# Fifth batch's x from two heads by 576 columns, weights of two steps converted in halves, new order

## Chip, cores and metric

One Trainium2 chip (trn2), one core. The metric is the device time of one execution in microseconds, median of three runs.

## What is computed

Attention for 8 batches of 8 heads (sequence 576, head size 64), with a softmax over the head size for q and over the sequence for k, then one MLP over all 4608 tokens:

```python
q_s = softmax(q, axis=-1); k_s = softmax(k, axis=2)     # max, exp, sum, division
kv = einsum('bhsd,bhse->bhde', k_s, v)
attn_out = einsum('bhsd,bhde->bhse', q_s, kv)
x = attn_out.transpose(0, 2, 1, 3).reshape(4608, 512)
h = x @ w_in                                            # 512 -> 2048
g = s * relu(h) ** 2 + b
out = g @ w_out                                         # 2048 -> 512
```

## The kernel before

All loops are unrolled. Each piece of work is a Python generator (a "stream") that yields an Op before each instruction group, with the engine, a modelled cost and what it needs, takes, frees and gives. A table, FIRST, is the order of the whole program: each number is the index of the stream whose next operation is issued. So FIRST sets the order on TensorE (PE), VectorE (DVE), ScalarE (ACT), GpSimd (POOL) and in SyncE's (SP) DMA queue, and every engine executes its own list in order.

The MLP runs in steps t = 16 * batch pair + f, over 16 slices f of the 2048. A step makes h (PE, L1868), relu (ACT, L1895), gh and gl (the high and the low part of g in fp32r; gl on DVE, L1905, L1914, L1921) and adds the products acc into the output (PE, L1942). Products are made with a high and a low part of each operand. From step 48 on, some products are combined Strassen-like: `early_sums` adds quarters of w_in (sum on DVE, stored as s_kept), and `differences_0` makes t1 to t4 (zone and t, DVE L1099 to L1110) from x of batches 4 and 6.

The attention runs in between. A pair pr is two units u = 2 pr + i of two heads each; four units are one batch, so batch 4 has u = 16 to 19, pairs 8 and 9. For batches 2 and above, `q_late` makes q's softmax and its transposed form qT, `kv_late` makes kv, `x_late` makes x. A pair is direct if its batch is below DIRECT: its q is cast to high and low parts (qhl or spare, all 128 partitions, one unit for both heads at once), kv becomes a block matrix of both heads, and x takes six matmuls (high by high, high by low, low by high; 320 and 256 columns, L934). For a pair that isn't direct, each head's high and low parts are packed into 128 partitions, with two DMAs qhl/spare<-qT (L840); x then takes one matmul per head and column part, and the two halves of partitions are added: a copy on ACT (L919), a sum on DVE (L923). `kv_late` normalises with two products (L884) for a direct pair and with four (L890) for another.

Batches 4 and 6 (PARK) are written to DRAM once x is known (xpark<-y) and come back as w<-xpark. `conv_w(f)` converts the weights of slice f to high and low parts by three operations of ACT and three of DVE, interleaved (low, clamp of st, prelu of st, low, cast w, difference w; L368 to L385), for w_in and w_out together (128x1024) or, for slice 0, apart (128x512). `fill` and `unused` (L2080) are matmuls of the identity with no use for the result, that the order table puts between products early on. mb is a per-column maximum, which goes through DRAM: sb (DVE) is stored as maxima and loaded as mb<-maxima for the k part of a batch.

For a pair that isn't direct, the branch of `x_late` that batch 4 now takes is:

```python
yield Op("PE", 0.57, begin(pr) + OFF_PE, needs=needs + free_x, take=["big", "sm"], gives=[f"xp{u}"], late=WAIT)
parts = [(xp[:, h, 0:L], xq[:, h * M:(h + 1) * M]) for h in range(2)]
for h in range(2):
    for a, n in enumerate((NT, NQ)):
        nc.tensor.matmul(parts[h][a], kvhl[:, h], qs[:, h, a, 0:n], start=True, stop=True)
for a in range(2):
    yield Op("ACT", (0.68, 0.67)[a], due, take=() if a else ["tmp"])
    for h in range(2):
        halves([(a, parts[h][a])], h)
for a in range(2):
    yield Op("DVE", (0.84, 0.7)[a], due, free=["big", "sm"] if a else (), gives=[f"y{u}"] if a else ())
    for h in range(2):
        sums_([(a, parts[h][a])], h)
```

Of the kernel before, what the change touches and what calls it, by code (L numbers as in the profile page):

```python
# [26 lines left out]
def attention_moe(ctx: ExitStack, tc: tile.TileContext, q, k, v, w_in, w_out, s, b, out):  # L27
# [6 lines left out]
    NFC = FF // P  # L34
# [7 lines left out]
    DUE_C0 = -60.0  # L42
# [101 lines left out]
    ON_ACT = (-1.0, -1.0, -1.0, -1.0, -1.0, 1.0, -1.0, -1.0, -1.0, 1.0, -1.0, 1.0, -1.0, 1.0, -1.0, 1.0)  # L144
    KN_ON = ('ACT', 'ACT', 'ACT', 'DVE')
    QF_ON = ('ACT', 'DVE', 'ACT', 'DVE', 'DVE', 'ACT', 'DVE', 'DVE')
    LESS_ON, OVER_ON = (1, 1, 1, 1, 1, 1, 1, 1), (1, 1, 1, 1, 0, 0, 0, 0)
    KT_IN = ("big", "acc") * 2
    BLOCKS_ON = [(("ACT", 1.03), ("DVE", 0.56))[i] for i in (1, 1, 0, 0)]
    WARM = 40  # L150
    IN_BIG = (1,)

    DUE_K = (-104.0, -52.5, -76.0, -79.5, 6.5, 28.5, 13.0, 38.5)
    DUE_Q = (-81.5, 70.0, -73.5, -18.0, 13.5, 2.0, -131.0, -33.5)
    DUE_V = (-26.0, -150.5, -207.0, -210.5)
    LATE_PR = (4, 5, 6, 7, 8, 9, 10, 11, 12, 13, 14, 15)
# [6 lines left out]
    PAIRS, ALONE, DIRECT = 3, 5, 5  # L163
# [19 lines left out]
    _, acc_low = banks("ps_acc0", "left")  # L183
    accs_open, acc_top = banks("ps_acc1", "left")
    two_banks, bigs = banks("ps_big", "right")
    free_accs = [acc_low, acc_top]
# [1957 lines left out]
```

## Time and profile before

| | |
|---|---|
| runs | 831.95, 830.03, 830.07 us |
| median | 830.07 us |
| profiled execution | 828.33 us, with a span of 826.5 us |
| PE busy | 818.7 us (99%) |
| DVE busy | 679.8 us (82%) |
| ACT busy | 531.0 us (64%) |
| granted TensorE clock | 1.00 (mean) |

The span goes from the first instruction to the last; the profiled execution has 1.8 us around it. Matmuls are pipelined, so a busy PE needn't be at its peak.

### The profile page before, as it was taken

To read this page: it belongs to the slowest core of one execution; us is meant where nothing else is said; L and a number is where in the kernel's file an instruction comes from. 1 tells how busy PE (TensorE), PEld (TensorE's weight loads), DVE (VectorE), ACT (ScalarE), POOL (GpSimd) and SP (SyncE) were. 2 spreads that over 40 slices of the span, in tenths; PEclk is the share of its full clock that TensorE was granted. 3 is DMA by queue.
4 is the path that set the end of the run, shared out by engine and by line. 5 is a ranking of instruction groups with operands and counts; after the bars stand their busy time and mean duration, and the time that the engine had idled before them with its cause. 6 is when DMAs were issued, how large, how long until landed. Compare 5 with 4: busy or idle time off the path is not lost.

```text
span 826.5 us, 12989 instructions
## 1 busy us (share of the span) xinstructions
PE 818.7 (99%) x4590; PEld 688.2 (83%) x4590; DVE 679.8 (82%) x1157; ACT 531.0 (64%) x931; POOL 25.3 (3%) x67
## 2 busy tenths in 40 slices
PE   8999999999999999999999999999999999999997
PEld 7787888888888888888888888888888888888997
DVE  6999997898888999989886898875555968789991
ACT  6899955455365456868886455765653457778950
POOL 5201000000000000000000000000000000000000
PEclk9999999999999999999999999999999999999999
DMA  9859235655896897888989987755469644453303
GB/s 313 314 174 364 60 90 146 197 136 192 257 322 185 261 211 227 230 263 233 252 260 313 327 281 222 226 182 175 147 244 345 228 161 149 176 178 115 110 20 102
DMA packets 152485, 173.41 MB, mean 210 GB/s; under 512 B 68836, under 2 KB 117476, under 8 KB 152292
## 3 DMA queue, kind: packets, MB, share of 16 engines
q1 hardware_dynamic: 151796, 171.99, 66.6%
q8 instruction: 36, 0.59, 0.3%
q10 hardware_dynamic: 624, 0.59, 0.2%
q14 instruction: 29, 0.24, 0.1%
HBM read 115.34 MB, written 43.04 MB: 192 GB/s over the span
## 4 chain that ended last, share of the span: by engine, by line
PE 93%; DVE 3%; DMA 2%; issue 1%; ACT 1%; SPq 0%; POOL 0%; ACTq 0%; DVEq 0%; POOLq 0%
PE acc L1942 35%; PE q L1323 24%; PE h L1868 13%; PE half_U L1764 6%; PE qa L1323 4%; PE half_A L1764 2%; DMA st<-in_moe_w_out_dram 2%; PE kv L474 1%; PE qa L1764 1%; PE xp L934 1%; PE b L1764 1%; PE b L474 1%; PE b L946 1%; PE kT L522 1%; PE xp L644 0%
## 5 line engine op out<-in xcount | busy, mean ns | idle before, releaser
L1942 PE MATMUL acc<-w,gh 128*128 128x512 f32 x880 | 273.5, 392 | 0.0
L1942 PEld LDWEIGHTS acc<-w,gh 128*128 128x128 f32 x880 | 162.6, 188 | 33.0 <-DVE o L1955 0.2
L1942 PE MATMUL acc<-w,gl 128*128 128x512 f32 x440 | 172.0, 391 | 0.1
L1868 PE MATMUL h<-x,w 128*128 128x512 f32 x576 | 143.8, 392 | 0.0
L1868 PEld LDWEIGHTS h<-x,w 128*128 128x128 f32 x576 | 106.8, 188 | 23.0 <-ACT r L1895 0.9
L1942 PEld LDWEIGHTS acc<-w,gl 128*128 128x128 f32 x440 | 82.6, 188 | 19.1 <-DVE gl L1921 1.1
L1323 PE MATMUL q<-w,w 128*128 128x512 f32 x376 | 95.6, 391 | 0.0
L1323 PEld LDWEIGHTS q<-w,w 128*128 128x128 f32 x376 | 70.0, 188 | 15.1 <-ACT r L1430 0.4
L1895 ACT ACTIVATE r<-h 128x512 f32<-128x512 f32 x48 | 28.6, 596 | 52.0 <-PE h L1868 49.7
L1430 ACT COPY zone<-q 128x512 f32<-128x512 f32 x32 | 18.7, 585 | 30.8 <-PE q L1323 29.8
L1432 DVE TENSOR_TENSOR zone<-q,zone 128x512 f32<-128x512 f32 x32 | 22.1, 690 | 19.0 <-ACT zone L1430 14.2
L1323 PE MATMUL q<-x,w 128*128 128x512 f32 x144 | 36.8, 391 | 0.0
L1323 PE MATMUL qa<-x,w 128*128 128x512 f32 x144 | 36.6, 389 | 0.0
L1323 PEld LDWEIGHTS qa<-x,w 128*128 128x128 f32 x144 | 27.0, 188 | 5.6
L1323 PEld LDWEIGHTS q<-x,w 128*128 128x128 f32 x144 | 26.8, 188 | 5.7
L1764 PE MATMUL half_U<-w 128*128 128x256 f32 x168 | 28.1, 283 | 0.0
L919 ACT COPY y<-b 64x320 f32<-64x320 f32 (+1 forms) x48 | 18.9, 394 | 11.4 <-PE b L946 10.6
L923 DVE TENSOR_TENSOR y<-b,y 64x320 f32<-64x320 f32 (+1 forms) x48 | 21.7, 453 | 5.4 <-ACT y L919 4.5
L1764 PEld LDWEIGHTS half_U<-w 128*128 128x128 f32 x168 | 24.1, 191 | 0.6
L1323 PE MATMUL q<-w,s 128*128 128x512 f32 x96 | 24.5, 391 | 0.0
L799 ACT ACTIVATE qe<-area 128x640 f32<-128x640 f32 x22 | 17.2, 787 | 10.3 <-DVE area L795 9.4
L1544 ACT CAST gh<-t 128x512 fp32r<-128x512 f32 x14 | 8.7, 624 | 23.1 <-PE acc L1942 23.1
(341 smaller groups left out, 1656.4 us busy)
## 6 DMA issues: line engine op xcount, KB each, us to landing
w<-w_kept SPq DMA_DIRECT2D x56, 512.0 KB, 5.5
st<-in_moe_w_in_dram SPq DMA_DIRECT2D x16, 512.0 KB, 8.0
st<-in_moe_w_out_dram SPq DMA_DIRECT2D x16, 512.0 KB, 8.4
w_kept<-w SPq DMA_DIRECT2D x16, 512.0 KB, 5.9
zone<-s_kept SPq DMA_DIRECT2D x16, 512.0 KB, 4.3
turned<-area SPq DMA_DIRECT2D x24, 320.0 KB, 3.5
qT<-turned SPq DMA_DIRECT2D x48, 160.0 KB, 3.5
area<-in_q_dram SPq DMA_DIRECT2D x14, 512.0 KB, 4.8
```

Source lines behind the costliest of these rows:

```text
L474: nc.tensor.matmul(kv[h * D:(h + 1) * D, i], kt[:, i, h, n], vt(2 * i + h, n), start=(n == 0), stop=(n == NT - 1))
L799: nc.scalar.activation(qe, qt_, AF.Exp)
L919: nc.scalar.copy(y[half[h], at[a]], x[half[1 - h]])
L923: nc.vector.tensor_tensor(out=y[half[h], at[a]], in0=x[half[h]], in1=y[half[h], at[a]], op=ALU.add)
L1323: nc.tensor.matmul(BANK[where], w(l)[:, c * P:(c + 1) * P], xs[m][:, c], start=k in (0, 1, 3) and n == 0, stop=n == 5, skip_group_check=True)
L1430: nc.scalar.copy(row(), BANK["U"])
L1432: nc.vector.tensor_tensor(out=row(), in0=BANK[("A", "B", "B")[n]], in1=row(), op=ALU.add)
L1544: nc.scalar.copy(gh, r)
L1764: nc.tensor.matmul(bank(where, j), g[:, js], w_, start=first and (j % 2 == 0 or k == 3) and n == 0, stop=bool(low), skip_group_check=True)
L1868: nc.tensor.matmul(hp_, w[:, j, c, :], x[:, c, :], start=(c == 0 and i == 0), stop=(c == NP - 1 and i == 2))
L1895: nc.scalar.activation(r, hp_, AF.Relu)
L1942: nc.tensor.matmul(acc[blk, j // 2][:, j % 2], g[:, js], w_, start=(f == 0 and i == 0), stop=(f == NFC - 1 and i == 2))
```

## The change

DIRECT goes from 5 to 4, so that batch 4's four units take the branch quoted above, with the two DMAs per unit and the four normalisation products per pair. HALVED lists the slices 1 and 2, whose weights are now converted in two halves: w_in first, w_out in a stream of its own at the end of the list (indices 669 and 670 in FIRST); its end waits until the first half has been read. The two banks for the products acc are taken in the other order. FIRST is rewritten to match: the order early on and in the stretch of batch 4; the rest has the same sequence. Of the table only its first lines are shown.

```diff
     FIRST = (
-        0, 18, 18, 0, 0, 18, 18, 20, 21, 46, 52, 19, 46, 46, 47, 2, 52, 46, 52, 3, 53, 46, 22, 47, 53, 52, 47, 52, 48, 46, 3, 68, 52, 53, 47, 52, 48, 4, 49, 47,
-        54, 4, 48, 55, 52, 54, 49, 68, 52, 55, 53, 49, 48, 29, 68, 49, 48, 29, 53, 49, 54, 53, 52, 29, 54, 52, 53, 69, 1, 29, 69, 55, 54, 53, 54, 29, 24, 52, 31, 53,
...
+        0, 18, 18, 0, 18, 0, 18, 20, 21, 46, 52, 19, 46, 46, 47, 2, 52, 46, 52, 22, 53, 46, 47, 53, 52, 47, 52, 3, 48, 46, 3, 68, 52, 53, 47, 52, 48, 49, 47, 24,
+        55, 48, 54, 52, 55, 49, 68, 52, 54, 53, 49, 48, 29, 68, 49, 48, 69, 29, 54, 53, 52, 49, 1, 53, 29, 54, 52, 4, 29, 53, 52, 4, 69, 55, 54, 23, 53, 54, 29, 55,
+        31, 53, 2, 29, 5, 31, 54, 53, 55, 69, 6, 72, 55, 54, 56, 5, 1, 31, 54, 53, 56, 1, 669, 57, 55, 54, 31, 25, 72, 32, 57, 55, 31, 54, 55, 56, 32, 669, 32, 72,
...
@@ -148,6 +149,7 @@
+    HALVED = (1, 2,)
@@ -160,7 +162,7 @@
-    PAIRS, ALONE, DIRECT = 3, 5, 5
+    PAIRS, ALONE, DIRECT = 3, 5, 4
@@ -183,7 +185,7 @@
-    free_accs = [acc_low, acc_top]
+    free_accs = [acc_top, acc_low]
@@ -373,7 +375,7 @@
-        yield Op("DVE", 1.13 * two + 0.03 * (n == 1), due, free=["w"] if last else (), gives=[f"w{f} {some.stop} read"], two=True)
+        yield Op("DVE", 1.13 * two + 0.03 * (n == 1), due, needs=[f"w{f} 1 read"] if last and n == 1 else (), free=["w"] if last else (), gives=[f"w{f} {some.stop} read"], two=True)
@@ -2092,7 +2094,7 @@
-            + [conv_w(0, slice(0, 1), DUE_C0), conv_w(0, slice(1, 2))] + [conv_w(f, slice(0, 2)) for f in range(1, NFC)]
+            + [conv_w(0, slice(0, 1), DUE_C0), conv_w(0, slice(1, 2))] + [conv_w(f, slice(0, 2 - (f in HALVED))) for f in range(1, NFC)]
@@ -2108,7 +2110,7 @@
-            + [exit_(n) for n in range(3)] + [exit_21()] + [exit_last(j) for j in (0, 2, 3)],
+            + [exit_(n) for n in range(3)] + [exit_21()] + [exit_last(j) for j in (0, 2, 3)] + [conv_w(f, slice(1, 2)) for f in HALVED],
```

On PE, in the early part of the program (h are products of a step, acc its output products, fill the matmuls without use, xp x of the first batch, qT and kT transposes), before:

```order
L1868 MATMUL h_406<-x_330,w_379 128x512 x3
L2080 MATMUL fill_444<-ident 128x128 x5
L644 MATMUL xp_450<-early,kvf 128x256
L644 MATMUL xp_450<-early,kvf 128x320
L2080 MATMUL fill_471<-ident 128x128 x9
L1868 MATMUL h_406<-x_330,w_379 128x512 x6
L2080 MATMUL fill_495<-ident 128x128 x4
L1868 MATMUL h_500<-x_330,w_468 128x512 x12
L2080 MATMUL fill_530<-ident 128x128 x6
L1942 MATMUL acc_0_537<-w_379,gh_491 128x512 x2
L1942 MATMUL acc_0_537<-w_379,gl_492 128x512
```

and after:

```order
L1870 MATMUL h_413<-x_329,w_386 128x512 x3
L2082 MATMUL fill_458<-ident 128x128 x3
L646 MATMUL xp_462<-early,kvf 128x256
L646 MATMUL xp_462<-early,kvf 128x320
L1870 MATMUL h_413<-x_329,w_386 128x512 x3
L2082 MATMUL fill_488<-ident 128x128 x9
L1870 MATMUL h_413<-x_329,w_386 128x512 x3
L1870 MATMUL h_505<-x_329,w_455 128x512 x6
L673 MATMUL kT_520<-ident,misc 128x128 x2
L1870 MATMUL h_505<-x_329,w_455 128x512 x6
L1870 MATMUL h_537<-x_329,w_503 128x512 x12
L1944 MATMUL acc_0_566<-w_386,gh_510 128x512 x2
```

Fill goes from four groups of 5, 9, 4 and 6 to two groups of 3 and 9; h of the second and third step come ahead of the first acc products.

On DVE, where the last parked unit of batch 4 is made (y its halves' sum, xp and xq the products in two buffers, sb the maxima that SP stores; gl_2935 belongs to step 41), before:

```order
L704 STREAM_TRANSPOSE misc<-misc 128x256
L709 TENSOR_REDUCE sb<-misc 128x8
L778 TENSOR_REDUCE qm_2950<-area 128x10
L795 TENSOR_TENSOR area<-area,qm_2950 128x640
L1910 TENSOR_SCALAR r_2933<-r_2933,sb 128x512
L1187 TENSOR_TENSOR sum_2937<-w_988 128x512
L802 TENSOR_REDUCE qs_2983<-qe_2975 128x20
L1914 TENSOR_TENSOR gl_2935<-r_2933,gh_2934 128x512
```

and after (gl_3044 belongs to step 42; lines are two higher than before):

```order
L706 STREAM_TRANSPOSE misc<-misc 128x256
L1919 SCALAR_TENSOR_TENSOR r_3042<-h_3002,sb,r_3042 128x512
L806 SCALAR_TENSOR_TENSOR qs_3037<-qs_3037 128x2x5
L811 RECIPROCAL qr_3060<-qs_3037 128x20
L804 TENSOR_REDUCE qs_3065<-qe_3030 128x20
L711 TENSOR_REDUCE sb<-misc 128x8
L925 TENSOR_TENSOR y_3050<-xp_3024,y_3050 64x320 x2
L1923 SCALAR_TENSOR_TENSOR gl_3044<-r_3042,sb,gh_3043 128x512
L925 TENSOR_TENSOR y_3050<-xq_3025,y_3050 64x256 x2
L806 SCALAR_TENSOR_TENSOR qs_3065<-qs_3065 128x2x5
```

sb has moved from ahead of gl of step 41 to between the gl of steps 41 and 42, right ahead of the four sums of the last y, with the gl of step 42 among these; before, y needed no operation of DVE.

In SP's queue, from the stores of batch 4 to the load w<-xpark for the second half of it, before:

```order
L430 DMA xleft<-misc 128x2x64
L714 DMA maxima_2973<-sb 128x4x2
L992 DMA xpark<-y_3009 128x4x64 x2
L1222 DMA zone<-s_kept 128x1024
L992 DMA xpark<-y_2964 128x4x64 x2
L719 DMA mb_3054<-maxima_2973 128x1024
L1074 DMA w_576<-xpark 128x1024
```

and after:

```order
L994 DMA xpark<-y_2969 128x4x64 x2
L716 DMA maxima_3075<-sb 128x4x2
L1032 DMA w_kept<-w_1042 128x1024
L994 DMA xpark<-y_3050 128x4x64 x2
L721 DMA mb_3113<-maxima_3075 128x1024
L432 DMA xleft<-misc 128x2x64
L1076 DMA w_588<-xpark 128x1024
```

mb<-maxima stands ahead of the load w<-xpark as before, but xleft<-misc moved behind it, to just ahead of w<-xpark, and the store of maxima stands behind the stores of one parked unit and ahead of those of the other, where it was ahead of both.

## Rows read from the trace of the kernel before

**Rows 1.** The page: busy time, share of the span, instructions of the engines.

```profile
PE 818.7 (99%) x4590; PEld 688.2 (83%) x4590; DVE 679.8 (82%) x1157; ACT 531.0 (64%) x931; POOL 25.3 (3%) x67
```

**Rows 2.** The chain of waits: share of the span by engine.

```profile
PE 93%; DVE 3%; DMA 2%; issue 1%; ACT 1%; SPq 0%; POOL 0%; ACTq 0%; DVEq 0%; POOLq 0%
```

**Rows 3.** Stretches: us, busy time of each engine, granted clock, DMA share, GB/s.

```profile
20.00:30.00 10.00, 9.72 (x65) 7.42 (x60) 9.96 (x18) 9.04 (x16) 5.74 (x9) 1.00 0.72 235
80.00:90.00 10.00, 9.95 (x45) 7.90 (x44) 10.00 (x14) 9.53 (x13) 0.40 (x2) 1.00 0.25 49
290.00:300.00 10.00, 10.00 (x46) 8.29 (x45) 9.75 (x16) 4.23 (x7) 0.00 (x0) 1.00 1.06 194
300.00:310.00 10.00, 10.00 (x46) 8.29 (x45) 8.73 (x14) 7.15 (x11) 0.21 (x2) 1.00 0.80 235
```

**Rows 4.** Timeline of PE, an x group: start, length, instructions.

```profile
255.26 0.96 PE L934 MATMUL xp<-qhl,spare 128*128 128x320 f32 x6
256.06 0.85 PE L1868 MATMUL h<-x,w 128*128 128x512 f32 x3
```

**Rows 5.** Groups by line: minimum, median, maximum ns, first and last start.

```profile
L923 DVE TENSOR_TENSOR y<-b,y x48: 406/437/496, 336.3 to 617.7; 64x320 f32<-64x320 f32 x24, 64x256 f32<-64x256 f32 x24
L919 ACT COPY y<-b x48: 363/396/425, 334.8 to 616.8; 64x320 f32<-64x320 f32 x24, 64x256 f32<-64x256 f32 x24
L982 ACT COPY y<-xp x4: 583/587/587, 259.3 to 288.1; 128x512 f32<-128x512 f32 x4
L837 ACT CAST qhl<-qhl x6: 723/726/727, 318.5 to 558.8; 64x640 fp32r<-64x640 f32 x6
```

**Rows 6.** Timeline of DVE around 281 to 319 us, idle time in brackets.

```profile
281.81 0.42 DVE L709 TENSOR_REDUCE sb<-misc 128x8 f32<-128x256 f32 x1
...
299.64 1.14 DVE L725 TENSOR_TENSOR mb<-mb 128x512 f32<-128x512 f32 x2
...
310.96 1.23 DVE L1106 TENSOR_TENSOR t<-w,w 128x1024 f32<-128x1024 f32 x1 [1.27 <-DMA s_kept<-sum]
...
318.92 0.74 DVE L1921 SCALAR_TENSOR_TENSOR gl<-r,sb,gh 128x512 fp32r<-128x512 f32 x1
```

**Rows 7.** Timeline of PE at step 46.

```profile
319.84 0.39 PE L1942 MATMUL acc<-w,gl 128*128 128x512 f32 x1
```

**Rows 8.** Timeline of the SP queue, 290 to 308 us.

```profile
290.23 3.51 SPq L992 DMA_DIRECT2D xpark<-y  x2
...
296.24 0.33 SPq L1074 DMA_DIRECT2D w<-xpark  x1
...
307.35 0.55 SPq L1195 DMA_DIRECT2D s_kept<-sum  x1
```

**Rows 9.** DMA issues: count, KB each, median us to landing.

```profile
mb<-maxima SPq DMA_DIRECT2D x12, 512.0 KB, 4.6
...
xpark<-y SPq DMA_DIRECT2D x16, 128.0 KB, 4.7
...
spare<-qT SPq DMA_DIRECT2D x12, 160.0 KB, 4.5
```

**Rows 10.** Groups of the tile maxima.

```profile
DMA to landing us min/median/max: 3.7/4.7/8.6
```

**Rows 11.** Timeline of PE, h of the second step and fillers.

```profile
30.33 3.03 PE L1868 MATMUL h<-x,w 128*128 128x512 f32 x12
33.19 0.82 PE L2080 MATMUL fill<-ident 128*128 128x128 f32 x6
33.76 0.71 PE L1942 MATMUL acc<-w,gh 128*128 128x512 f32 x2
```

**Rows 12.** Groups of the conversion by line (128x512 and 128x1024 together).

```profile
L372 DVE TENSOR_SCALAR st<-st x17: 409/684/896, 16.2 to 91.3; 128x1024 f32<-128x1024 f32 x15, 128x512 f32<-128x512 f32 x2
L378 DVE SCALAR_TENSOR_TENSOR low<-st,low x17: 670/1215/1226, 18.8 to 102.1; 128x1024 uint32<-128x1024 uint32 x15, 128x512 uint32<-128x512 uint32 x2
```

**Rows 13.** Timeline of ACT, a wait for w_out.

```profile
34.77 1.17 ACT L368 ACTIVATE low<-st 128x1024 int32<-128x1024 uint32 x1 [0.58 <-DMA st<-in_moe_w_out_dram]
```

186 rows, old and new, of the table FIRST are left out of this document.

## Prediction

> **What bounds the kernel now.** I read the page's busy times first. TensorE (PE) is busy for 99% of the span and VectorE (DVE) for 82% [rows 1], and the chain that ended last lies on PE for 93% of the span, on DVE for 3%, on DMA for 2% [rows 2]. So the first question for each edit is what it takes from PE, and the second is whether DVE, or a DMA in SyncE's (SP) queue, then makes PE wait. A share of 82% hides that DVE has stages of its own, and the busy time by stretches shows them: of 10 us DVE is busy 9.96 from 20 to 30 us and 10.00 from 80 to 90 (there the weights are converted), 9.75 from 290 to 300 and 8.73 from 300 to 310 [rows 3]. The granted clock is 1.00 in each. In the first and the last of these stages PE and DVE are full together, so a saving on PE alone needn't shorten them. The edits fall into just these two: a new early order with two conversions in halves, and x of batch 4.
>
> **x of batch 4, on PE.** Before, a unit's x is six matmuls; from their first start to the start of the next group it is 256.06 - 255.26 = 0.80 us [rows 4]. The new form has four of the same six (two of 320 columns, two of 256): 0.53. For four units that is 4 x 0.27 = 1.07 us less PE work, in a stretch in which PE has no idle time, so it counts in full unless another wait takes its place.
>
> **x of batch 4, on DVE and ScalarE (ACT).** The two heads' products now lie in different halves of the partitions. Per unit ACT makes four copies of 64 partitions, 4 x 0.396 = 1.58 us, and DVE four sums, 4 x 0.437 = 1.75 (medians of the batches that are built so already); ACT also casts 64x640, 0.726, and loses the copy of 128x512, 0.587 [rows 5]. Four units: DVE +7.0, ACT +6.9. The key normalisation has two small products more per pair on DVE, for which I take half a sum each: +1 in all, bounds 0 and +1.7 (a whole sum each). DVE gets some 8 us more within 60. From 290 to 310 it has only 20 - 18.48 = 1.5 us free [rows 3], so the 8 must be absorbed before, out of idle time and out of the reserve with which gl (an operand of the acc products) is ready before PE wants it. That reserve is smallest just behind, at step 46: gl starts at 318.92, takes 0.74, so ends at 319.66 [rows 6], and PE starts on it at 319.84 [rows 7]: 0.18 us.
>
> On these halves the Trainium skill speaks against the change: "Perfetto Trace Analysis", section "Partition Dimension", wants a tile's first dimension to be 128 except in special cases, and these tiles have 64. The trace agrees with it: 0.396 us for 64x288 elements on the mean is 21 ps for each, against 9 ps in the copy of 128x512 [rows 5]. If time went by elements, four copies would take 0.66 us, ACT's +6.9 would be +3.2, and the result nearer to the rival in which the gains are kept.
>
> **What a later y sets back.** Batch 4 is parked in DRAM and comes back as w<-xpark for the sums t1 to t4 on DVE. Before, the last y is a copy on ACT that starts at 288.1 [rows 5]; the last stores are issued from 290.23 to 293.74, and w<-xpark follows at 296.24 [rows 8]. Behind it in SP's queue stand w_kept, five loads of v, turned, two qT and the store s_kept<-sum at 307.35 [rows 8]; for the buffer of this store t (t3) on DVE waited 1.27 us, until 310.96 [rows 6]. From there DVE has no wait up to gl of step 46. So this is a chain by which a late y reaches PE. After the change the last y needs four copies (288.1 + 1.58 = 289.7) and four sums (1.75) on DVE, with r, a reduction, gl (0.74) and small ones among them: ready at 291.5 to 293.1, in the times of before. The store lands a median of 4.7 us after its issue [rows 9], so w<-xpark goes out between 296.2 and 298. I take +0.8 us; bounds 0 and +2.0. Second, maxima<-sb follows sb, which DVE made at 281.81 [rows 6] and now makes just ahead of the last y's sums, about 290; ahead of w<-xpark in SP's queue stand mb<-maxima, as before, and now xleft too. With the median landing of 4.7 [rows 10], mb<-maxima goes out at about 295 and delays nothing more. Its maximum is a rival, below. The eight new stores qhl/spare<-qT stand in SP's queue by 160 KB each, ahead of the same loads; a median landing of 4.5 [rows 9] is what each x waits for once more, and since the order starts these units' q early enough to hide it I cost it at nothing; if it isn't hidden, PE waits for xp by up to that.
>
> **The early order.** 12 matmuls of fill less, 2 of unused more: ten less. Six took 33.76 - 33.19 = 0.57 us [rows 11], so ten are 0.95. They stood where PE would have waited, so leaving them out gains only if other products are ready. They are: h of step 1 (30.33 to 33.19) is followed by h of step 2, and acc of step 0 begins some 2.7 us later than before, when its gl is long ready. The bound then is DVE. It must do more: a conversion in halves takes 2 x 0.409 for 0.684 and 2 x 0.670 for 1.215, and a third operation like the second [rows 12], so up to 0.4 us more per step, 0.8 for both; the shorter ones overlap at their ends, so half of it is the lower end, +0.4. Against that DVE has only 0.04 us of idle time to lose from 20 to 30 [rows 3]. ACT stood 0.58 us for w_out at 34.77 [rows 13], and w_out of that step now is issued earlier, since xleft moves behind it on SP. I take -0.8, which is the fillers less a part for the conversion; bounds 0 (DVE full throughout) and -1.5 (fillers and ACT's wait).
>
> **The sum.** PE comes to step 46 ahead by 0.8 + 1.07 = 1.87 us. But gl of step 46 comes, against before, by +0.8 for w<-xpark and -0.8 for the early part, which moves everything: 0.0. The reserve of 0.18 is used up, so PE starts there 0.2 us earlier than before and the other 1.7 us are a wait. Behind it PE has no slack to the end, so -0.2 stays: 828.33 - 0.2 = 828.1 on the profiled execution's scale. The median of the runs shown, 830.07, is 1.74 above that execution: 829.9.
>
> **Rivals.** (a) All gains are kept: t3 no longer waits for s_kept<-sum, or the y sums come early enough (DVE's extra 8 us absorbed by 290). Then -1.87, 828.2; with the bounds, -1.1 to -2.6. For it: DVE waited 1.27 us there, which shows slack on DVE itself. Against: the queue's order behind xpark is unchanged. It decides if t3 starts more than 1.5 us before 310.96. (b) Slower: maxima<-sb takes its maximum, 8.6 us [rows 10], as it may behind the 512 KB of w_kept now ahead. Then mb<-maxima goes out at 299 and, landing 4.6 later [rows 9], lets the mb product on DVE start at 303.5, not 299.64 [rows 6]; r, gl and t3 stand behind it on DVE, and w<-xpark goes out 3.5 later as well: 3.7 - 0.18 - 0.8 = +2.7, 832.8. It decides from about 2 us of lateness of that mb product. A half of it gives +1.0, 831.1. (c) The early part gives nothing, DVE being full: -0.2 + 0.8 = +0.6, 830.7. (d) The clock: with fewer fillers PE could stand for a moment near 28 to 36 us, and a granted clock at 1.2 in place of 2.4 GHz would double the products of, say, that step's h: +2.9 by its 33.19 - 30.33 [rows 11]; the rows show only 1.00 [rows 3]. The Trainium skill, "TensorE: Matmul & The Clock Gate", section "HAM oscillation — how this bites in real kernels", has an idle PE fall back to the lower level; no run shown here has it.
>
> **How the numbers follow.** About 0.3%, 2.5 us, is what a measurement of this kernel can tell from no change. Chances: the forecast with (c) 0.50; (a) 0.28; (b) in full 0.09, by half 0.09; (d) 0.02; another 0.02 for a larger gain. Faster by over 0.3%: the far end of (a), 0.06, and the 0.02, so 0.08 or, rounded up for what I can't see, 0.10. Slower: full (b) and (d), 0.11. Same: 0.79. The range holds (a) down to 827.9 and half of (b) up to 832.0; about 0.1 lies out on either side.
>
> **What the changed kernel's profile would show.** Right: x as groups of four, 0.53 us; acc of step 0 within 0.3 us after h of step 2; acc 0.5 to 1.5 earlier than before from 60 to 230 us; t3 on DVE 0 to 1 us before 310.96, still waiting for s_kept<-sum; PE waiting 1 us or more for gl by step 46. Wrong: xp or h waiting over 0.5 us between 235 and 300; DVE waiting for mb<-maxima; no wait at step 46.

## The result and the profile after

The changed kernel takes 835.17 us (median of 8 runs, 832.87 to 837.46), the kernel before, run beside it on the same chip, 830.19 (8 runs, 828.59 to 831.95). The ratio is 1.0058, with a 95% interval of 1.0044 to 1.0072: 4.8 us slower. The forecast was 829.9, with a range up to 832.0.

The profiled execution took 833.72 us with a span of 831.9, 5.39 more than the one of before. The page's busy times and its chain of waits, as in [rows 1, 2]:

```profile
PE 818.6 (98%) x4572; PEld 685.8 (82%) x4572; DVE 686.5 (83%) x1183; ACT 538.9 (65%) x953; POOL 25.0 (3%) x67
...
PE 84%; DMA 5%; DVE 3%; SPq 3%; ACT 2%; issue 1%; ACTq 0%
```

PE's busy time is that of before, with 18 matmuls fewer; DVE got 6.7 us more and ACT 7.9. What is new is that PE no longer makes up the chain alone: 84% of it against 93%. The stretches of 10 us, with the columns of [rows 3], say where (in the last row PE was busy 10.00 before):

```profile
250.00:260.00 10.00, 9.18 (x43) 7.32 (x42) 8.19 (x17) 7.22 (x13) 0.00 (x0) 1.00 0.78 237
...
290.00:300.00 10.00, 10.00 (x46) 8.23 (x46) 9.84 (x18) 5.32 (x9) 0.00 (x0) 1.00 0.89 186
300.00:310.00 10.00, 8.73 (x37) 6.59 (x36) 9.02 (x14) 5.24 (x9) 0.00 (x0) 1.00 0.71 192
```

PE's waits by what it waited for (us in total, times, longest). The kernel before had only two:

```profile
PE unused L2080 <- POOL ident masks.py:199: 2.5, 1, 2.5
PE xp L644 <- DVE early L636: 0.3, 1, 0.3
```

The changed kernel has nine:

```profile
PE unused L2082 <- POOL ident masks.py:199: 2.5, 1, 2.5
PE q L1325 <- ACT zone L1432: 1.7, 1, 1.7
PE h L1870 <- DVE r L1919: 0.9, 2, 0.5
PE acc L1944 <- ACT gh L1921: 0.8, 1, 0.8
PE acc L1944 <- DVE gl L1916: 0.8, 1, 0.8
PE xp L967 <- DMA qhl<-qT: 0.5, 1, 0.5
PE acc L1944 <- DVE gl L1923: 0.5, 1, 0.5
PE xq L967 <- DVE y L925: 0.3, 1, 0.3
PE h L1870 <- DVE w L387: 0.2, 1, 0.2
```

PE's timeline has these waits in three places, 250 to 266 us, 306 to 323, and 428:

```profile
251.00 0.41 PE L967 MATMUL xp<-qhl,spare 128*128 128x320 f32 x1 [0.48 <-DMA qhl<-qT]
...
258.84 0.35 PE L967 MATMUL xq<-spare 128*128 128x256 f32 x1 [0.34 <-DVE y L925]
...
265.27 3.02 PE L1870 MATMUL h<-x,w 128*128 128x512 f32 x12 [0.34 <-DVE r L1919]
...
278.51 0.32 PE L967 MATMUL xp<-qhl,spare 128*128 128x320 f32 x1
...
279.05 2.20 PE L1870 MATMUL h<-x,w 128*128 128x512 f32 x9
...
306.35 0.50 PE L1944 MATMUL acc<-w,gl 128*128 128x512 f32 x1 [0.76 <-DVE gl L1916]
...
309.46 3.01 PE L1870 MATMUL h<-x,w 128*128 128x512 f32 x12 [0.52 <-DVE r L1919]
...
321.64 0.73 PE L1944 MATMUL acc<-w,gh 128*128 128x512 f32 x2 [0.82 <-ACT gh L1921]
...
322.82 0.50 PE L1944 MATMUL acc<-w,gl 128*128 128x512 f32 x1 [0.45 <-DVE gl L1923]
...
428.71 1.65 PE L1325 MATMUL q<-w,w 128*128 128x512 f32 x6 [1.75 <-ACT zone L1432]
```

Setting PE's start on gl in the acc products of a step beside the same step of before gives a running account. These are steps 32 and 43, in before and then in after:

```profile
231.50 0.39 PE L1942 MATMUL acc<-w,gl 128*128 128x512 f32 x1
...
300.61 0.39 PE L1942 MATMUL acc<-w,gl 128*128 128x512 f32 x1
```

```profile
229.73 0.39 PE L1944 MATMUL acc<-w,gl 128*128 128x512 f32 x1
...
299.99 0.39 PE L1944 MATMUL acc<-w,gl 128*128 128x512 f32 x1
```

At step 32 PE is 1.77 us ahead. From there to step 43 it takes 70.26 us against 69.11, though x should be 1.07 shorter, so 2.2 us are lost. The three waits up to 266 us that are listed make 1.2 of them; the rest goes in smaller pieces around them and behind. From step 43 to step 46 it takes 22.83 against 19.23, 3.60 more: step 46 starts at 322.82 against 319.84 [rows 7], 2.98 late. At 424 us another 2.0 go, and the end is 5.4 late.

The stage after 300 is one chain, which runs through ACT, DVE and SP. ACT's last copy for the last parked y, and DVE's rows (start, length, idle time before in brackets):

```profile
288.83 0.75 ACT L921 COPY y<-xq 64x256 f32<-64x256 f32 x2
```

```profile
290.79 0.40 DVE L711 TENSOR_REDUCE sb<-misc 128x8 f32<-128x256 f32 x1
291.11 0.98 DVE L925 TENSOR_TENSOR y<-xp,y 64x320 f32<-64x320 f32 x2
292.12 0.75 DVE L1923 SCALAR_TENSOR_TENSOR gl<-r,sb,gh 128x512 fp32r<-128x512 f32 x1
292.90 0.86 DVE L925 TENSOR_TENSOR y<-xq,y 64x256 f32<-64x256 f32 x2
...
304.13 1.23 DVE L1105 TENSOR_TENSOR zone<-w,zone 128x1024 f32<-128x1024 f32 x1 [0.87 <-DMA w<-xpark]
...
314.07 1.22 DVE L1108 TENSOR_TENSOR t<-w,w 128x1024 f32<-128x1024 f32 x1 [2.79 <-DMA s_kept<-sum]
...
322.02 0.74 DVE L1923 SCALAR_TENSOR_TENSOR gl<-r,sb,gh 128x512 fp32r<-128x512 f32 x1
```

And the SP queue behind it:

```profile
292.22 1.93 SPq L994 DMA_DIRECT2D xpark<-y  x2
...
298.46 0.33 SPq L1076 DMA_DIRECT2D w<-xpark  x1
...
308.84 1.27 SPq L827 DMA_DIRECT2D qT<-turned  x2
310.20 0.55 SPq L1197 DMA_DIRECT2D s_kept<-sum  x1
```

Read from the top: the copies end at 289.58, but DVE has no idle time from 284 to 303 us and comes to the four sums only at 291.11. They end at 293.76, the last store goes out at 293.79, and w<-xpark, for which SP waits until that store has landed, is issued 4.67 later, at 298.46, 2.22 later than before [rows 8]. The lateness then stays: the store s_kept<-sum +2.85 [rows 8], t3 +3.11 and gl of step 46 +3.10 [rows 6], PE +2.98 [rows 7]. In before the last store went out nearly as late, at 293.23, since SP needed 2.96 us to issue the one ahead of it; but it landed in 2.96. So of the 2.22 us some 0.6 is the store's later issue and 1.7 its longer way to the landing.

### The profile page after: what moved, and what is told of

The parts are those of the page before. It is cut to its first block, busy times and chain, and to the rows that moved or that the text cites. A ratio compares the mean times of both kernels' runs of the same rounds, so it can differ in the third digit from the quotient of the medians.

```text
span 831.9 us, 13038 instructions
## 1 busy us (share of the span) xinstructions
PE 818.6 (98%) x4572; PEld 685.8 (82%) x4572; DVE 686.5 (83%) x1183; ACT 538.9 (65%) x953; POOL 25.0 (3%) x67
## 4 chain that ended last, share of the span: by engine, by line
PE 84%; DMA 5%; DVE 3%; SPq 3%; ACT 2%; issue 1%; ACTq 0%
PE acc L1944 32%; PE q L1325 23%; PE h L1870 12%; PE half_U L1766 6%; PE qa L1325 4%; PE half_A L1766 2%; PE qa L1766 1%; PE kv L476 1%; PE b L1766 1%; SPq L462 1%; PE b L476 1%; DMA spare<-qT 1%; PE b L948 1%; PE xp L936 1%; DMA w<-xpark 1%
## 5 line engine op out<-in xcount | busy, mean ns | idle before, releaser
L1921 ACT ACTIVATE gh<-r,sb 128x512 fp32r<-128x512 f32 x25 | 18.0, 721 | 10.4 <-DVE r L1919 10.4
```

The source lines that it names most:

```text
L1921: nc.scalar.activation(gh, r, AF.Identity, bias=b_col)
```

## Experiments

Two theories were set against each other. **A**: SP's in-order queue behind the late y (the stores, w<-xpark, s_kept<-sum) makes the loss. **B**: DVE simply has too much work from 236 to 310 us, wherever y stands. After the runs, a table has the account of each profile. Many edits move one number in FIRST: 524 is the store s_kept<-sum, 204 q of unit 20 with its qT<-turned, 240 x of unit 19, 209 q of unit 25 with spare<-qT, 470 the load w<-xpark. Of a line of FIRST only the part that changes is shown, and of longer edits only the lines that tell what they do. Unless said, times are medians and the ratio is to the kernel before, with its interval.

**The early part alone, and the late part alone.** The first has the early order and both halved conversions, with batch 4 as before; the second the reverse.

```diff
...
-    PAIRS, ALONE, DIRECT = 3, 5, 4
+    PAIRS, ALONE, DIRECT = 3, 5, 5
```

> The new early order and the two conversions in halves, with batch 4's x and everything from 232 us on as before. Both theories (A: a late last y of batch 4 holds back SP's queue up to the store s_kept<-sum and t3 waits for its buffer; B: DVE simply has too much work from 235 to 300 us): the lead of PE that the changed kernel has from 60 to 230 us, 1.5 to 1.8 us, stays to the end, since the queue and DVE behind it only move along: 1.5 to 1.8 us faster than before. If DVE or a DMA in 290 to 320 us is bound by something that doesn't move along, less.

> Batch 4's x from two heads, with the order from 232 us on of the changed kernel, and the early order and the whole conversions of before. Both theories: the whole loss and no early lead, 5.0 + 1.6 = 6.6 us slower than before; the start of t3 on DVE at about 315.8 us. If the early order matters to the loss, not additive.

The early part alone takes 830.41 us, ratio 1.0005 (0.9990 to 1.0021): no gain, against the 1.5 and more that was expected. The lead was there, 1.0 us at step 32 and 0.85 at step 43, and went to 0.42 at step 46. The place is the one of [rows 6], as this kernel's DVE row shows:

```profile
310.67 1.23 DVE L1107 TENSOR_TENSOR t<-w,w 128x1024 f32<-128x1024 f32 x1 [1.84 <-DMA s_kept<-sum]
```

PE comes earlier, but t3 only by 0.3 us: DVE waits 1.84 us there where it waited 1.27 in before. In this profile the rest went at 424 us, in a wait of 1.9 us, which the kernel before can have too, as its second profile shows below. The late part alone takes 835.82, ratio 1.0064 (1.0044 to 1.0084), 4.7 us behind at step 46: the loss lies wholly in batch 4. This run has the new form of x together with the new order from 232 us on, and no run parts the two. w<-xpark is issued at 295.27 in the first of these kernels and at 299.92 in the second, against 296.24 before [rows 8]: the early part brings it forward by 1.0, batch 4 sets it back by 3.7.

**The store ahead of qT<-turned in SP's queue**, in the kernel after and in the kernel before:

```diff
-        117, 274, 116, 204, 162, 117, 118, 181, 118, 117, 524, 180,
+        117, 274, 116, 524, 204, 162, 117, 118, 181, 118, 117, 180,
```

> The changed kernel with one move in SP's queue: the store s_kept<-sum (of the seventh sum) goes ahead of the two loads qT<-turned, for which SP waits until 308.84 us. Theory A: the store is issued at about 306.1 instead of 310.20, t3 no longer waits 2.79 us for it and starts at about 311.3; of the 5.0 us slower, 2.0 to 2.8 are gone. Theory B: DVE has the same work, so 0.5 us at the most.

> The kernel before with the same move in SP's queue. t3 starts at about 309.7 instead of 310.96 us. Both theories: PE waited for nothing there, so 0 to 0.3 us faster.

After with it takes 833.87, ratio 1.0043 (1.0029 to 1.0058): 1.3 us less than after, which the intervals do not separate. t3 starts at 312.54 without a wait, so the queue did hold it; but in that execution DVE waited earlier for w<-xpark, 1.61 us until 305.45. Before with it takes 829.92, ratio 0.9993 (0.9981 to 1.0005), though t3 starts at 309.24, 1.7 us earlier: there PE wasn't waiting for it.

**The kernel before once more**, unchanged, with a profile:

> The kernel before, unchanged, for a second profile. In the profiles of the changed kernel and of four variants PE waits 0.9 to 2.0 us for ACT near 424 us, behind a late landing of spare<-qT, and in the one profile of before it doesn't. If that wait belongs to the change, it is absent here again. If it belongs to this DMA's varying landing, whatever the kernel (4.5 us in the first profile, 5.6 to 6.7 in the others), it is here too, 1 to 2 us, and about 2 us of the difference between the first profiles isn't the change's.

It took 834.4 us, 4 above its own median. The largest of PE's new waits, and the stretch from 425 us with the columns of [rows 3]:

```profile
PE q L1323 <- ACT zone L1430: 1.8, 1, 1.8
```

```profile
425.00:435.00 10.00, 8.16 (x30) 6.34 (x29) 6.01 (x10) 7.73 (x26) 0.00 (x0) 0.83 0.55 170
```

So the wait at 424 us is not the change's own. The granted clock of this stretch is 0.83 (1.00 in the first profile), and from 415 to 445 us this execution lost 3.7 us against that one.

**y earlier on DVE**: the four sums ahead of the qs operations; and the same together with the store's move and gl of step 44 ahead of t2.

```diff
-        113, 240, 204, 113, 205, 114, 115, 162, 240, 162, 115, 406, 114, 115, 240, 115, 205,
+        113, 240, 162, 240, 240, 114, 114, 204, 113, 205, 115, 115, 162, 406, 115, 115, 205,
```

> The changed kernel with sb, the four sums of the last y and gl of step 42 ahead of three small operations and a reduction of q on DVE, so that the last y is ready at about 291.9 instead of 293.76 us. Theory A (queue chain): w<-xpark goes out at 296.5 to 297 instead of 298.46, so the wait of t2 for it (0.87) is gone, t3 starts 1.5 to 2 us earlier (312.1 to 312.6), and the time falls by 1 to 2 us. Theory B (DVE has too much work): the same work, so no change beyond 0.5 us.

> The changed kernel with the last y early as in the run before, the store s_kept<-sum ahead of qT<-turned, and gl of step 44 ahead of t2 (which waits for w<-xpark). Theory A: no wait in the queue chain is left that reaches PE; acc of step 46 no longer waits; of what the changed kernel loses from 300 to 322 us (3.6 us) some 3 are gone: 3 us faster than the changed kernel, 832. Theory B: 0.5 to 1.

They take 834.00, ratio 1.0043 (1.0026 to 1.0060), and 833.63, ratio 1.0038 (1.0023 to 1.0053). The last stores went out at 293.66 and 292.48, yet w<-xpark at 299.17 and 297.90, 5.5 and 5.4 us behind, not 4.67 as in after: SP still waited for the store's landing, 1.0 and 0.7 us, with mb<-maxima and xleft already issued. So in the second the store was 1.3 us earlier than in after and the load only 0.6. With all three moves the wait on PE only changed its name:

```profile
PE h L1870 <- DVE r L1919: 2.4, 2, 2.1
```

**More work for DVE in the kernel before**: ten reductions of q are added, 7.2 us of DVE's busy time, with y as before.

```diff
-        nc.vector.tensor_reduce(out=qm, in_=qt, axis=AX.X, op=ALU.max, negate=bool(on_act))
+        for _ in range({18: 2, 19: 3, 20: 2, 21: 2}.get(u, 1)):
+            nc.vector.tensor_reduce(out=qm, in_=qt, axis=AX.X, op=ALU.max, negate=bool(on_act))
...
+            for _ in range({18: 2, 19: 3, 20: 2, 21: 2}.get(u, 1)):
+                nc.vector.tensor_reduce(out=qs, in_=qe, axis=AX.X, op=ALU.add)
```

> The kernel before with ten reductions of q of units 18 to 21 repeated on DVE (each writes the same values again), 7.4 us more DVE work from 247 to 290 us, while y stays a copy on ACT. Theory A: y, its stores and w<-xpark stay where they are, so no more than 1 us slower, and t3's start moves by less than 1 us. Theory B: as much DVE work as the change brings, so 3 us slower or more.

It takes 835.45, ratio 1.0069 (1.0042 to 1.0095). PE waits 2.0 us for x at 257 us, 0.8 for gl at 291 and 0.7 for r at 294, and loses 4.95 from step 32 to step 43. So as much DVE work as the change adds costs as much as the change by itself: A, which gave it 1 us at most, falls as the whole cause. But the loss stands in another place: only 0.6 us of it falls from step 43 to 46, where the change loses 3.6. The run shows that DVE is full here, and not that the change loses its time in the same way.

**Less work for DVE in the kernel after; no wait for the last y; both.** The first leaves out q's maximum and its subtraction in units 18 to 21. The second lets the load for the second half read the first, which is parked long before, so that the second half of batch 4 is left out of t2 to t4, and has the store's move.

```diff
-        nc.vector.tensor_reduce(out=qm, in_=qt, axis=AX.X, op=ALU.max, negate=bool(on_act))
+        if u not in (18, 19, 20, 21):
+            nc.vector.tensor_reduce(out=qm, in_=qt, axis=AX.X, op=ALU.max, negate=bool(on_act))
...
```

```diff
-        nc.sync.dma_start(home(2 + i).bitcast(F32), xpark[a, :, 2 * i:2 * i + 2])
+        nc.sync.dma_start(home(2 + i).bitcast(F32), xpark[a, :, 2 * i * a:2 * i * a + 2])
...
```

> The changed kernel without the maximum of q and its subtraction before the exponential in units 18 to 21 (left out: part of the softmax that only guards against overflow): eight operations of 128x640, 0.74 us each from start to start, so 5.9 us less DVE work from 247 to 290 us, nothing moved. Theory B (too much DVE work): the waits of PE from 236 to 322 us go, 3 to 4 us faster than the changed kernel, 831 to 832. Theory A alone (the queue behind the last y): the y sums come up to 1 us earlier, 1 us faster at the most.

> The changed kernel with the second load w<-xpark right behind the first, reading the first half's rows again (left out: the second half of batch 4 in the sums t2 to t4, so that nothing waits for the last y's stores), and the store s_kept<-sum ahead of qT<-turned. No wait in SP's queue for y is left, and DVE has the same work. Theory A: all of the loss after 300 us goes, 3.0 to 3.6 us faster than the changed kernel, 831.5 to 832. Theory B: no more than the run with the store alone, 1.3 us.

> The changed kernel with both taken out: no maximum of q and subtraction in units 18 to 21 (left out), and the second w<-xpark reading the first half again (left out: the second half of batch 4 in t2 to t4) with s_kept<-sum ahead of qT<-turned. If A and B together are all of the loss after 300 us: PE has no wait from 300 to 325 us, is level with the kernel before there (the rest of the early lead and x's saving went into 2.2 us of waits from 236 to 300), and the time is that of before within 0.7 us, 830 to 831.

The three take 833.14, ratio 1.0037 (1.0018 to 1.0057); 832.33, ratio 1.0022 (1.0006 to 1.0037); and 831.00, ratio 1.0004 (0.9991 to 1.0018). Against after, the second and the third gain more than the intervals leave open (3.0 and 4.5 us by the ratios); the first, 1.7, doesn't quite. From step 43 to step 46 they lose 1.8, 1.4 and 1.7 us where after loses 3.6: each alone brings back some 2 us, and both together no more. (Of the second's 2.2 us the store's move by itself, e3_after_store_up, brought 1.0.) In the third profile what is late there is what rival (b) named, DVE's wait for the maxima, which landed 6.5 us after their issue, against 4.8 in after; in the second it is 0.3 us, in the first there is none:

```profile
302.26 1.15 DVE L727 TENSOR_TENSOR mb<-mb 128x512 f32<-128x512 f32 x2 [1.11 <-DMA mb<-maxima]
```

**The early part with the store's move**, batch 4 as before:

> The early order and the halved conversions alone (batch 4 as before), and the store s_kept<-sum ahead of qT<-turned. Theory A: the early lead of 1.0 to 1.8 us, of which the wait at step 46 left 0.3 to 0.4 without the move, stays to the end: 1 to 1.5 us faster than the kernel before, 829. Theory B: the same, since DVE has room there.

It takes 829.16, ratio 0.9984 (0.9971 to 0.9998). PE has no wait at step 46 and loses nothing from step 43 on. But in this profile PE waited 0.6 us for ACT at 253 us, its lead was down to 0.1 at step 43, and at 424 us came a wait of 2.0.

**The kernel after once more**, unchanged, with a profile:

> The changed kernel, unchanged, for a second profile: PE's waits between 236 and 325 us are the same in place and within 0.5 us in size (they belong to the program), and the wait near 424 us and any lower granted clock differ (they belong to the execution).

837.86 us, and the same waits at the same places, so the first profile was typical of the change. The wait at 424 is larger, and the granted clock behind it (430 to 440 us) 0.76 to 0.90:

```profile
PE q L1325 <- ACT zone L1432: 3.4, 1, 3.4
...
PE xp L967 <- DMA qhl<-qT: 1.1, 1, 1.1
PE acc L1944 <- DVE gl L1916: 1.0, 1, 1.0
```

**The wait at 424 taken away**: spare<-qT of unit 25 is issued ahead of the DMAs w<-w_kept, r_kept<-zone and zone<-s_kept, in the kernel before and in the kernel after (in the latter the number to move stands further down the table).

```diff
-        298, 320, 245, 210, 298, 422, 320, 244, 320, 298, 322, 210, 320, 298, 280, 322, 281, 210, 322, 209,
+        298, 320, 245, 210, 298, 209, 422, 320, 244, 320, 298, 322, 210, 320, 298, 280, 322, 281, 210, 322,
```

> The kernel before with the two DMAs spare<-qT of unit 25 ahead of w<-w_kept, r_kept<-zone and zone<-s_kept in SP's queue (their data is there from 409.9 us, and they were issued at 415.91). They are issued at about 411.5 and land by 417, so ACT doesn't wait for the buffer near 421 us and PE not near 424: 1 to 2 us faster than the kernel before, with fewer executions above 831.

> The changed kernel with the same move. If the wait near 424 us belongs to the execution: as much faster as in the kernel before, plus the part by which it is larger here; the difference between the two kernels with the move is what the profiles show at 325 us, 3.0 to 3.7 us. If the difference of 4.8 us stays, another cause stands behind 424 us.

Before so takes 828.66, ratio 0.9975 (0.9964 to 0.9986); after so 832.37, ratio 1.0018 (1.0004 to 1.0032), with PE 3.9 us late at step 46 in its profile and no wait at 424. Set against each other they give 1.0018 / 0.9975 = 1.0043, with some 0.0018 to either side: the change costs 3.6 us where this wait can't add to it.

**The early part with both moves**, batch 4 as before:

> The early order and the halved conversions with batch 4 as before, the store s_kept<-sum ahead of qT<-turned, and spare<-qT of unit 25 ahead as in the two runs before: the early lead of 1.3 us and the wait near 424 us, 1 to 2, together: 827 to 828.

It takes 827.14 (826.70 to 827.71), ratio 0.9955 (0.9943 to 0.9967): 3.7 us faster than the kernel before and 8.6 than the changed one. The move of spare<-qT by itself gave 2.1 of the 3.7 (e13_before_spare_up, 0.9975), so the early part with the store's move adds some 1.7, as the ratio of the two has it. PE's waits in it, all of them:

```profile
PE unused L2081 <- POOL ident masks.py:199: 2.5, 1, 2.5
PE h L1869 <- DVE w L386: 0.2, 1, 0.2
```

**The account of the profiles.** PE against the first profile of before, in us: how far ahead at step 32, and what it took more from there to step 43 (69.11 before) and on to step 46 (19.23 before).

| kernel | ahead at step 32 | 32 to 43 | 43 to 46 |
|---|---|---|---|
| before, second profile | -0.6 | +0.9 | +0.7 |
| e4, e13 (old order) | 0.4, 1.0 | 0.0, 0.0 | 0.0, +0.8 |
| e1, e11, e15 (early part) | 1.0, 1.0, 0.9 | +0.2, +0.9, 0.0 | +0.4, 0.0, 0.0 |
| e2 (late part) | 0.3 | +1.0 | +4.0 |
| after, its second profile, e14 | 1.8, 1.9, 1.0 | +1.2, +1.9, +1.2 | +3.6, +3.6, +3.7 |
| e3, e6, e7 (moves in after) | 1.5, 0.9, 1.4 | +1.5, +2.0, +1.3 | +2.6, +3.3, +4.0 |
| e9, e10, e16 (parts out) | 1.2, 1.4, 2.1 | +1.1, +1.5, +1.9 | +1.8, +1.4, +1.7 |
| e8 (DVE's load, old order) | 0.8 | +5.0 | +0.6 |

The loss from step 32 to 43 is in every kernel with the new batch 4, 1.0 to 2.0 us, and no edit here took it away. Two profiles with the old batch 4, the second of before and e11's, lose 0.9 there too, so a part of it may belong to the execution. The one from 43 to 46 yields to edits of the queue and of DVE's work alike.

## Why the prediction was wrong

**What held.** x is a group of four, 279.05 - 278.51 = 0.54 us (0.53 predicted), so PE's work is less by the 1.07 us. Only two of the four groups run so; the two that wait, at 250 and 258 us, take 1.27 and 1.12 to the start of the next group, more than the 0.80 of before. The copies and sums cost what [rows 5] gave, 0.37 to 0.42 and 0.42 to 0.49 us. The copies of the last y end at 289.58 (289.7 predicted), but by luck: 289.7 was in the times of before, and here PE had come 1.77 us ahead. A sum of 64x256 takes DVE as long as one of 128x256, 0.42 us each (L702 and L701, at 287.52 and 287.07). The Trainium skill, "Perfetto Trace Analysis", section "Partition Dimension", wants 128 there, and these rows agree with it. acc of step 0 starts right behind h of step 2 (35.76 us). The early part's 0.8 holds: at step 32 the twelve profiles that have it are 0.9 to 2.1 us ahead, 1.3 on the mean, and the six with the old order -0.6 to 1.0, 0.3 on the mean. That it isn't kept past step 46 was predicted too, and e1_early_only, which loses 0.4 there, and e11_early_store_up, which loses nothing, show the place.

**The step that failed is "What a later y sets back".** Its term was +0.8 us with bounds 0 and +2.0, on w<-xpark in the times of before; e2_late_only, which has only this part, measures +3.7. The mechanism, y to w<-xpark to the queue to t3 to gl, was right, the landing of 4.7 us too (4.67), and the early part moved the load by the 0.8 that was set against it (1.0 in e1_early_only). What was mis-sized is when y is ready: 291.5 to 293.1 was predicted, and e2_late_only's last sum ends at 295.1. There ACT starts the copies 1.2 us later than I took (289.27 for 288.1), and 1.6 us lie between their end (290.88) and the first sum (292.43), since DVE, without a moment of idle time, has a reduction for qs, r and sb ahead of it:

```profile
290.14 0.74 ACT L919 COPY y<-xq 64x256 f32<-64x256 f32 x2
```

```profile
292.43 0.98 DVE L923 TENSOR_TENSOR y<-xp,y 64x320 f32<-64x320 f32 x2
...
294.22 0.86 DVE L923 TENSOR_TENSOR y<-xq,y 64x256 f32<-64x256 f32 x2
```

```profile
299.92 0.33 SPq L1074 DMA_DIRECT2D w<-xpark  x1
```

I counted what stands among the four sums, and not the queue that the full engine had in front of them. In the sum, gl of step 46 was put at 0.0 against before; in after it comes 3.10 later, and PE starts on it 2.98 late, not 0.2 early.

**"The 8 must be absorbed before" was named, but not priced.** The prediction saw 1.5 us of room from 290 to 310 and let the rest be taken up out of idle time and reserve. e8_before_dve_load shows a price: 7.2 us of DVE work in this stretch cost 5 us in the kernel before, with nothing else changed, if mostly ahead of step 43. The runs so fit A and B as the two ends of one chain: full DVE makes y late, and the queue carries the lateness on to t3, r and gl. That this is all of the loss is not shown. Each end eased alone brings back some 2 of the 3.6 us from step 43 to 46. The time of e16_after_both_out is that of the kernel before; but of the 4.5 us that it gains on after, its profile places only 1.9 here, and where the others lie is open.

**"I cost it at nothing" for qhl/spare<-qT failed too.** PE waited for it, 0.5 us in one profile of after and 1.1 in the other, within the bound named (4.5), and some more for y and r behind it; from step 32 to 43 after lost 2.2 us in all, 2.9 in its second profile. The landing is not hidden for the first of these units. No run here took away this wait alone, so how much of the 2.2 hangs on it stays open.

**The rivals.** (a), all gains kept, needed t3 1.5 us before 310.96; it came 3.1 behind. (b), the maxima, did not happen in after: they landed in 4.8 us and DVE didn't wait for them. Its place is real all the same: mb's product started 1.4 us later than before, and in e16_after_both_out DVE waited 1.1 us for the maxima. (c) is half true: the early part alone gives nothing, but not because DVE is full at 30 us; at step 32 its lead was there, 1.0 us, and it went later. (d) did not happen at 28 to 36 us: the granted clock from 20 to 40 us is 1.00.

**What the prediction had no term for** is the wait at 424 us, where ACT waits for spare<-qT and so PE for zone. It was 1.7 and 3.4 us in the two profiles of after, none and 1.8 in those of before, and without it the change costs 3.6 instead of 4.8. The difference of 1.2 is within what the intervals of the two ratios leave open, so whether the change itself makes this wait longer stays unsettled. The profiles only show that the DMA takes longer to land (6.3 and 6.6 us in after, 4.5 and 6.5 in before), not why.

## What to carry to other kernels

Where PE and a second engine are full together, price what is added to the second engine by its own free time in that stage, and list every instruction that stands ahead of the new ones there, not only those of the step in mind. A lead that one engine has gained can be worth nothing until the next store or load in an in-order queue that the stage waits for has been moved too: the early order alone gave 0 (ratio 1.0005), and with two DMAs moved some 1.7 us beyond the 2.1 that one of the moves gives by itself. A wait that isn't in the one profile at hand can still be in the median; profile the kernel before twice.

## What the runs showed of the hardware

A wait of about 2 us on PE can cost nearly as much again. In e5_before_again, e6_after_y_early and e12_after_again the granted clock was lower behind the wait at 424 us, of 1.8, 2.7 and 3.4 us (0.83 from 425 to 435 us in the first, 0.69 and 0.76 from 430 to 435 in the others), and in e7_after_all behind a wait of 2.06 us that ended at 310.43, where twelve products of h then took 4.61 us (3.01 in after). Its stretches:

```profile
305.00:310.00 5.00, 3.37 (x15) 2.44 (x13) 4.43 (x7) 3.09 (x5) 0.00 (x0) 1.00 0.76 229
310.00:315.00 5.00, 4.57 (x13) 3.62 (x14) 4.46 (x6) 2.09 (x3) 0.40 (x2) 0.66 0.73 226
...
311.10:314.40 3.30, 3.30 (x10) 2.52 (x9) 3.24 (x5) 1.40 (x3) 0.40 (x2) 0.50 0.63 188
```

The Trainium skill, "TensorE: Matmul & The Clock Gate", section "HAM oscillation — how this bites in real kernels", has an idle PE fall back to the lower of the two levels; these rows agree: in the last of them, right behind the wait, the granted clock is 0.50, which is 1.2 GHz of 2.4. It is not so behind every wait: in the first profile of after, the stretches of 5 us from 425 to 440 all show 1.00, behind one of 1.75 us, and so do those of e10_after_no_park_wait, behind one of 2.33.

A DMA's way from issue to landing differs between executions of one kernel by 2 us: spare<-qT, for which ACT waits at 424 us, took 4.5 us in the first profile of before and 6.5 in its second. Where the change decides, at the last store of y, the two profiles of a kernel lie closer: 2.96 and 3.3 us in before; in both of after the load that waits for it goes out 4.67 behind it.
